# Fourier mixing folded over the model axis twice: smaller DFT products, the middle column apart

## The chip, the cores and the metric

The kernel runs on one core of a Trainium2 chip. The metric is device time in microseconds; it is compared over several runs of the same program. Engines are named as in the profile: PE (TensorE matmul) and PEld (its weight load), DVE (VectorE), ACT (ScalarE), POOL (GpSimd), SP (SyncE, here only a DMA queue).

## The reference

Eight batches of random-feature attention (8 heads, 576 rows, head size 64, 128 features), whose output x (8 x 576 x 512) goes through Fourier mixing, a layer norm and two channel products.

```python
q_p, k_p = phi(q * scale), phi(k * scale)       # phi: exp(h - max(h)), h = x @ omega.T - |x|^2 / 2
kv  = einsum('bhsm,bhsd->bhmd', k_p, v);  z = sum(k_p, axis=2)
x   = (q_p @ kv) / (q_p @ z + 1e-6)             # heads side by side: (8, 576, 512)
u   = x + real(fft(fft(x, axis=1), axis=2))
un  = (u - mean(u)) / sqrt(var(u) + 1e-6)
out = u + maximum(un @ w_ch1, 0) @ w_ch2        # 512 -> 2048 -> 512
```

The real part of the two-dimensional transform of a real x is C x C' - S x S', where C and S are the cosine and sine matrices over the sequence, and C' and S' those over the model axis. Cosines are even and sines odd in their index, both over the sequence (t and 576 - t) and over the model axis (d and 512 - d).

## The kernel before, in words

**Layout.** x of a batch is one tile of 97 partitions x 6 x 512. Sequence rows are kept as pairs: three chunks of "lo" rows t = 0 to 288 and three of "hi" rows 576 - t, chunks sharing their border rows. So x[:, 0:3] + x[:, 3:6] is the even part over the sequence and x[:, 0:3] - x[:, 3:6] the odd one.

**Stages of a batch.** `attn` computes four pairs of heads in 32 steps; its last step writes x's last columns from ndp (line 299). `mix` follows in 13 steps. For each block of 128 columns (dc = 0 to 3), DVE makes the even fold and POOL the odd one (line 321), six matmuls multiply them with the sequence tables cs and sn (yp, line 326, N = 289), and ACT copies the result to y (line 333). Then, for each of three chunks of rows, eight matmuls multiply y with the model tables cd and sd (ab, line 343, N = 257): only the columns 0 to 256 are computed, A from the even part and B from the odd part, since A - B is the transform at column k and A + B the one at 512 - k. ACT copies B (line 352), DVE forms A - B and A + B (lines 353, 354), POOL adds them to x (lines 358, 359; the right half reads them backwards), DVE and POOL make the layer norm (lines 363 to 371), PE transposes the rows (tp, line 382) and turns the hi rows round (fp, line 396). `mlp` runs the two channel products twice per batch, over lo and over hi rows: hp (line 411) and op (line 430), all with N = 289; then it transposes back (otp, line 446), adds (line 452) and stores.

**Order of the work.** The functions are generators. `together` advances the channel products of batch b as the main line, in 38 steps, and the attention and mixing of batch b + 1 beside it, in 45 steps (32 + 13), so that the mixing falls to the second half of the hi products: there each main step is a group of 8 op matmuls. Before that, the weights are loaded (64 pieces, given as doubles and narrowed to f32 by DVE and POOL, their DMAs issued from POOL's queue), with the attention and mixing of batch 0 beside them. The last batch's channel products have nothing beside them. Instructions keep this order by priority, each engine running its own queue in order; where an instruction isn't ready by the planner's own estimate, a later one is taken ahead.

**Buffers.** Scratch tiles are handed out from pools by tag. The fold tile before uses the tag "ke" of the attention (2 buffers), which "un" uses too; y is one buffer; the tiles of the hidden layer, ht, have 18 buffers, 16 of which one half-batch fills.

Of the kernel before, what the change touches and what calls it, by code (L numbers as in the profile page):

```python
# [12 lines left out]
AF = mybir.ActivationFunctionType  # L13
ALU = mybir.AluOpType
# [19 lines left out]
def _tables(S, DM):  # L34
    """The DFT matrices in the layouts of the two contractions."""
# [8 lines left out]
    d = 128 * np.arange(DM // 128)[None, :] + np.arange(128)[:, None]  # L44
    turn = (d[:, :, None] * np.arange(DM // 2 + 1)) % DM
    ang = 2.0 * np.pi * turn / DM
    cd = np.cos(ang)
    sd = np.where(turn * 2 % DM == 0, 0.0, np.sin(ang))
# [7 lines left out]
def kernel(  # L56
# [20 lines left out]
    KD = DM // 2 + 1  # L77
    R = 6
# [3 lines left out]
    # Both feature maps carry 1 / sqrt(MF); left out of both, it scales the term  # L82
    # that is added to the denominator.
# [68 lines left out]
        # the magnitude, within the range of float32  # L152
# [4 lines left out]
        # exponent - 1023 + 127 in eight bits  # L157
# [24 lines left out]
    # omega^T, once for each head of a pair  # L182
# [32 lines left out]
    def attn(b):  # L215
        x = xs[b] = xp.tile([CP, R, DM], F32, name="x", tag="x")
        for pr in range(NP):
# [9 lines left out]
            # q in the order of the pairs: lo t = 0 .. 288, hi t = 0 .. 288  # L227
# [37 lines left out]
            for i in range(2):  # L265
# [38 lines left out]
                )  # L304
                yield

# [1 line left out]
    uns = {}  # L308

    def mix(b):  # L310
# [207 lines left out]
```

## Time and profile before

| | |
|---|---|
| time, median of 3 runs (lowest to highest) | 1860.35 us (1859.08 to 1861.77) |
| span of the profiled execution (its only time shown) | 1856.5 us |
| instructions | 21861 |
| PE busy | 1752.1 us (94%), 9137 matmul instructions |
| PEld busy | 1409.8 us (76%) |
| DVE busy | 639.6 us (34%) |
| ACT busy | 358.2 us (19%) |
| POOL busy | 208.7 us (11%) |
| mean granted PE clock | 0.969 |

A row of the groups reads: line, engine, operation, out <- in by tile names, shapes, count, busy time and mean duration in ns, then the engine's idle time just before these instructions and what ended it. A row of the timeline reads: start, length, engine, line, operation, how many instructions are merged, and the idle time before. Matmuls are pipelined, so that durations overlap; distances between starts give the pace. Pool spans are rough.

### The profile page before, as it was taken

How to read it: one execution, taken by the hardware profiler on the slowest of the kernel's cores; microseconds unless marked ns; L12 is line 12 of the kernel's file. 1: busy time of each engine (PE TensorE's matmuls, PEld its weight loads, DVE VectorE, ACT ScalarE, POOL GpSimd, SP SyncE). 2: the span in 40 equal slices, each digit the busy share in tenths (PEclk: the TensorE clock that was granted, in tenths of full speed). 3: DMA queues.
4: the chain of work that ended last, by engine and by line, in shares of the span. 5: the costliest groups of instructions: out<-in, count | busy, mean ns of one | idle time of the engine just before them, and what ended most of it. 6: DMA issues, size and time to landing. Idle time of an engine off the chain costs nothing.

```text
span 1856.5 us, 21861 instructions
## 1 busy us (share of the span) xinstructions
PE 1752.1 (94%) x9137; PEld 1409.8 (76%) x9137; DVE 639.6 (34%) x1450; ACT 358.2 (19%) x641; POOL 208.7 (11%) x319
## 2 busy tenths in 40 slices
PE   5997988999999899999999999998999999998998
PEld 5885766877888688877888678886888778886776
DVE  5777873313242323313233132413233132332000
ACT  1221121112121212212221121212122121211100
POOL 2335331010001200011001100012000110012000
PEclk9997978999999999999999999999999999999999
DMA  6322322001110101101010011101011010000000
GB/s 145 82 79 71 93 76 55 7 1 26 26 45 7 26 20 29 24 7 26 20 40 20 9 24 23 43 7 26 20 33 26 1 26 20 20 1 13 1 13 13
DMA packets 125013, 57.73 MB, mean 31 GB/s; under 512 B 115762, under 2 KB 115762, under 8 KB 124916
## 3 DMA queue, kind: packets, MB, share of 16 engines
q1 hardware_dynamic: 119248, 37.83, 8.7%
q0 software_dynamic: 5120, 16.78, 2.8%
q10 hardware_dynamic: 548, 1.73, 0.4%
q8 instruction: 73, 1.20, 0.3%
q14 instruction: 24, 0.20, 0.0%
HBM read 46.88 MB, written 9.44 MB: 30 GB/s over the span
## 4 chain that ended last, share of the span: by engine, by line
PE 82%; DVE 7%; POOL 4%; DMA 4%; issue 2%; ACT 1%; POOLq 0%; SPq 0%; DVEq 0%; ACTq 0%
PE hp L411 26%; PE op L430 24%; PE yp L326 5%; PE kvp L269 5%; PE kp L245 4%; PE qp L254 4%; PE ndp L295 4%; PE ab L343 4%; DMA raw<-in_moe_w_ch_dram 4%; PE eps L280 2%; POOL x L359 1%; PE fp L396 1%; PE tp L382 1%; PE tps L194 1%; PE otp L446 1%
## 5 line engine op out<-in xcount | busy, mean ns | idle before, releaser
L430 PE MATMUL op<-ht,w 128*128 128x289 f32 x2048 | 531.7, 413 | 8.2 <-POOL w L170 8.2
L411 PE MATMUL hp<-unT,w 128*128 128x289 f32 x2048 | 532.5, 414 | 0.0
L430 PEld LDWEIGHTS op<-ht,w 128*128 128x128 f32 x2048 | 387.5, 192 | 116.9 <-POOL w L170 9.5
L411 PEld LDWEIGHTS hp<-unT,w 128*128 128x128 f32 x2048 | 387.0, 193 | 114.7 <-issue 8.7
L420 DVE TENSOR_SCALAR ht<-hp 128x289 f32<-128x289 f32 x128 | 58.8, 459 | 374.6 <-PE hp L411 374.6
L254 PE MATMUL qp<-omT,qT 64*97 64x128 f32 x768 | 112.1, 299 | 15.8 <-DVE qT L238 14.6
L245 PE MATMUL kp<-omT,kT 64*96 64x128 f32 x768 | 114.5, 302 | 5.3 <-DVE ke L206 2.9
L254 PEld LDWEIGHTS qp<-omT,qT 64*97 64x97 f32 x768 | 100.5, 182 | 22.8 <-issue 15.9
L245 PEld LDWEIGHTS kp<-omT,kT 64*96 64x96 f32 x768 | 98.5, 180 | 25.4 <-issue 17.9
L422 ACT ACTIVATE ht<-hp 128x289 f32<-128x289 f32 x128 | 52.8, 412 | 296.7 <-PE hp L411 296.7
L269 PEld LDWEIGHTS kvp<-v,ke 96*128 96x128 f32 x768 | 103.5, 209 | 6.9 <-issue 1.1
L269 PE MATMUL kvp<-v,ke 96*128 96x65 f32 x768 | 105.3, 291 | 0.0
L212 ACT ACTIVATE ke<-ke 96x768 f32<-96x768 f32 x64 | 53.8, 841 | 213.5 <-DVE ke L206 213.5
L295 PEld LDWEIGHTS ndp<-kv,qeT 128*97 128x97 f32 x768 | 82.3, 180 | 10.3 <-ACT qeT L286 2.0
L353 DVE TENSOR_TENSOR bmp<-ab,bmp 97x257 f32<-97x257 f32 x24 | 10.2, 423 | 221.4 <-ACT bmp L352 221.4
L204 DVE TENSOR_REDUCE kemx<-kp 96x6 f32<-96x768 f32 x64 | 60.8, 950 | 70.4 <-PE kp L245 70.4
L295 PE MATMUL ndp<-kv,qeT 128*97 128x65 f32 x768 | 82.6, 262 | 1.6 <-DVE kv L277 1.3
L452 DVE TENSOR_TENSOR x<-x,otp 97x512 f32<-97x512 f32 x48 | 32.5, 683 | 148.6 <-PE otp L446 148.6
L113 POOL MEMSET v<- 96x12 f32 x32 | 3.7, 116 | 700.6 <-PE kvp L269 694.0
L286 ACT ACTIVATE qeT<-eps 128x582 f32<-128x582 f32 x64 | 42.0, 656 | 192.9 <-PE eps L280 174.2
L321 POOL TENSOR_TENSOR fold<-x 97x384 f32<-97x384 f32 x32 | 40.1, 1252 | 331.7 <-PE kvp L269 242.2
L440 ACT ACTIVATE ot<-op 128x289 f32<-128x289 f32 x64 | 26.4, 412 | 255.4 <-PE op L430 255.4
(65 smaller groups left out, 1558.8 us busy)
## 6 DMA issues: line engine op xcount, KB each, us to landing
raw<-in_moe_w_ch_dram POOLq DMA_DIRECT2D x64, 256.0 KB, 3.0
kn<-in_k_dram SPq DMA_DIRECT2D x64, 144.0 KB
qn<-in_q_dram SPq DMA_DIRECT2D x64, 144.0 KB
v<-in_v_dram SPq DMA_DIRECT2D x64, 144.0 KB
out_dram<-x SPq DMA_DIRECT2D x40, 192.0 KB
out_dram<-x SPq DMA_DIRECT2D x8, 190.0 KB
cd_sb<-k_cd ACTq DMA_DIRECT2D x1, 385.5 KB
sd_sb<-k_sd ACTq DMA_DIRECT2D x1, 385.5 KB
```

What stands on the lines that cost most here:

```text
L204: nc.vector.tensor_reduce(mx[:], pr4, axis=AX.X, op=ALU.max)
L212: nc.scalar.activation(out=e[:], in_=e[:], func=AF.Exp, scale=SCALE)
L245: nc.tensor.matmul(kp[0:PR, r // 3, r % 3 * MF : r % 3 * MF + MF], lhsT=kT[rows, r, :], rhs=omT[rows, :],)
L254: nc.tensor.matmul(qp[0:CP, r // 3, r % 3 * MF : r % 3 * MF + MF], lhsT=qT[rows, t0 : t0 + CP], rhs=omT[rows, :],)
L269: nc.tensor.matmul(kvp[:, 0 : D + 1], lhsT=kes[i][:, r, :], rhs=v1[:, i, r, :], start=(r == 0), stop=(r == R - 1),)
L295: nc.tensor.matmul(nd[:, r, :], lhsT=qeT[:, r, :], rhs=kv[:])
L326: nc.tensor.matmul(yp[:, 0:NK], lhsT=f[:, c, :], rhs=tab[:, c, :], start=(c == 0), stop=(c == NC3 - 1),)
L343: nc.tensor.matmul(ab[0:CP, n, 0:KD], lhsT=y[:, n, dc, CW * c : CW * c + CP], rhs=tab[:, dc, :], start=(dc == 0), stop=(dc == NDC - 1),)
L411: nc.tensor.matmul(hp[:, 0:NK], lhsT=w1[:, dc, 128 * fc : 128 * fc + 128], rhs=un_t[:, dc, :], start=(dc == 0), stop=(dc == NDC - 1),)
L420: nc.vector.tensor_scalar(ht[:], hp[:, 0:NK], 0.0, None, op0=ALU.max)
L422: nc.scalar.activation(out=ht[:], in_=hp[:, 0:NK], func=AF.Relu)
L430: nc.tensor.matmul(op_[:, 0:NK], lhsT=w2[:, fc, 128 * dc : 128 * dc + 128], rhs=hs[fc][:], start=(fc == 0), stop=(fc == NFC - 1),)
```

## The change

The model axis is folded as well, and twice. First, the even part over the sequence is added to its mirror image over the model axis (columns 1 to 255 with 511 to 257), and the odd part has its mirror image subtracted: this leaves 257 columns. Second, column d is combined with column 256 - d, once added and once subtracted: one combination is enough for the even result columns k, the other for the odd ones. So there are four folds of 128 columns (n = 0 to 3: cosine for even k, cosine for odd k, sine for even k, sine for odd k), and both contractions run over 128 columns instead of 512.

- The sequence products become 4 x 3 matmuls of N = 289 instead of 8 x 3.
- The model products become, per chunk, one matmul each for A and B and for even and odd k, of N = 129 or 128 and without accumulation, instead of eight of N = 257.
- Column 128 is its own partner (256 - 128) in the second fold. For the sine part it takes the place of column 0 (which is zero there). For the cosine part it is carried apart in `mid_t`, multiplied with cs in three matmuls of N = 1 per chunk, and lands in column 257 of the sine bank; it is added to A for k a multiple of 4 and subtracted for k = 2 modulo 4.
- The tables cd and sd have their columns sorted (k = 0 mod 4, 2 mod 4, odd) and 128 rows instead of 512. DVE puts the columns back in order as it forms A - B and A + B: six instructions with strided results instead of two.
- The folds of a batch are now made at once, on the whole x: first all of DVE's, then all of POOL's, in two steps; the sequence products follow in two more steps, so that the count of 13 stays. Both engines use the one buffer of the scratch tile "half".
- ht has 17 buffers instead of 18, and fold has a buffer of its own.

```diff
-    d = 128 * np.arange(DM // 128)[None, :] + np.arange(128)[:, None]
-    turn = (d[:, :, None] * np.arange(DM // 2 + 1)) % DM
-    ang = 2.0 * np.pi * turn / DM
-    cd = np.cos(ang)
-    sd = np.where(turn * 2 % DM == 0, 0.0, np.sin(ang))
+    d = np.arange(DM // 4)[:, None]
+    k = np.arange(DM // 2 + 1)
+    k = np.concatenate([k[k % 4 == 0], k[k % 4 == 2], k[k % 2 == 1]])[None, :]
+    turn = (d * k) % DM
+    cd = np.cos(2.0 * np.pi * turn / DM)
+    turn = (np.where((d == 0) & (k % 2 == 1), DM // 4, d) * k) % DM
+    sd = np.where(turn * 2 % DM == 0, 0.0, np.sin(2.0 * np.pi * turn / DM))
...
+    QD = DM // 4
+    KE = QD + 1
+    K0 = DM // 8 + 1
...
-        y = fft.tile([128, 2, NDC, NK], F32, name="y", tag="y")
-        for dc in range(NDC):
-            cols = slice(128 * dc, 128 * dc + 128)
-            fold = att.tile([CP, 2, NC3, 128], F32, name="fold", tag="ke")
-            for n, (tab, eng, op) in enumerate(
-                ((cs, nc.vector, ALU.add), (sn, nc.gpsimd, ALU.subtract))
-            ):
-                f = fold[:, n]
+        fold = fft.tile([CP, NC3, 4, QD], F32, name="fold", tag="fold")
+        mid_t = small.tile([CP, NC3, 1], F32, name="mid", tag="mid", bufs=2)
+        for n, (eng, op, back) in enumerate(
+            ((nc.vector, ALU.add, ALU.add), (nc.gpsimd, ALU.subtract, ALU.subtract))
+        ):
+            h = fft.tile([CP, NC3, DM], F32, name="half", tag="half")
+            eng.tensor_tensor(out=h[:], in0=x[:, 0:NC3, :], in1=x[:, NC3:R, :], op=op)
+            eng.tensor_tensor(
+                out=h[:, :, 1 : 2 * QD],
+                in0=h[:, :, 1 : 2 * QD],
+                in1=h[:, :, DM - 1 : 2 * QD : -1],
+                op=back,
+            )
+            even, odd = (ALU.subtract, ALU.add) if n else (ALU.add, ALU.subtract)
+            for m, o in ((0, even), (1, odd)):
                 eng.tensor_tensor(
-                    out=f, in0=x[:, 0:NC3, cols], in1=x[:, NC3:R, cols], op=op
-                )
-                yp = sml.tile([128, 512], F32, name="yp", tag="sml")
-                for c in range(NC3):
-                    nc.tensor.matmul(
-                        yp[:, 0:NK],
-                        lhsT=f[:, c, :],
-                        rhs=tab[:, c, :],
-                        start=(c == 0),
-                        stop=(c == NC3 - 1),
-                    )
-                nc.scalar.activation(out=y[:, n, dc, :], in_=yp[:, 0:NK], func=AF.Copy)
+                    out=fold[:, :, 2 * n + m, :],
+                    in0=h[:, :, 0:QD],
+                    in1=h[:, :, 2 * QD : QD : -1],
+                    op=o,
+                )
+            middle = fold[:, :, 3, 0:1] if n else mid_t[:]
+            eng.tensor_copy(out=middle, in_=h[:, :, QD : QD + 1])
             yield
+
+        y = fft.tile([128, 4, NK], F32, name="y", tag="y")
+        for n, tab in enumerate((cs, cs, sn, sn)):
+            yp = sml.tile([128, 512], F32, name="yp", tag="sml")
+            for c in range(NC3):
+                nc.tensor.matmul(
+                    yp[:, 0:NK], lhsT=fold[:, c, n, :], rhs=tab[:, c, :],
+                    start=(c == 0), stop=(c == NC3 - 1),
+                )
+            nc.scalar.activation(out=y[:, n, :], in_=yp[:, 0:NK], func=AF.Copy)
+            if n % 2:
+                yield
...
             ab = big_tile("ab")
+            rows = slice(CW * c, CW * c + CP)
             for n, tab in enumerate((cd, sd)):
-                for dc in range(NDC):
+                for m, cols in enumerate((slice(0, KE), slice(KE, KD))):
                     nc.tensor.matmul(
-                        ab[0:CP, n, 0:KD],
-                        lhsT=y[:, n, dc, CW * c : CW * c + CP],
-                        rhs=tab[:, dc, :],
-                        start=(dc == 0),
-                        stop=(dc == NDC - 1),
-                    )
-            bmp = att.tile([CP, 3, KD], F32, name="bmp", tag="qe")
+                        ab[0:CP, n, cols], lhsT=y[:, 2 * n + m, rows], rhs=tab[:, cols]
+                    )
+            for i in range(NC3):
+                nc.tensor.matmul(
+                    ab[0:CP, 1, KD : KD + 1], lhsT=cs[:, i, rows], rhs=mid_t[:, i, :],
+                    start=(i == 0), stop=(i == NC3 - 1),
+                )
+            bmp = att.tile([CP, 3, KD + 1], F32, name="bmp", tag="qe")
             bs, mi, pl = (bmp[:, n, :] for n in range(3))
-            nc.scalar.activation(out=bs, in_=ab[0:CP, 1, 0:KD], func=AF.Copy)
-            nc.vector.tensor_tensor(out=mi, in0=ab[0:CP, 0, 0:KD], in1=bs, op=ALU.subtract)
-            nc.vector.tensor_tensor(out=pl, in0=ab[0:CP, 0, 0:KD], in1=bs, op=ALU.add)
+            nc.scalar.activation(out=bs, in_=ab[0:CP, 1, 0 : KD + 1], func=AF.Copy)
+            mid = bmp[:, 0, KD : KD + 1]
+            for dst, op in ((mi, ALU.subtract), (pl, ALU.add)):
+                for first, c0, c1, sign in ((0, 0, K0, ALU.add), (2, K0, KE, ALU.subtract)):
+                    nc.vector.scalar_tensor_tensor(
+                        dst[:, first:KD:4], ab[0:CP, 0, c0:c1], mid, bs[:, c0:c1], op0=sign, op1=op
+                    )
+                nc.vector.tensor_tensor(
+                    out=dst[:, 1:KD:2], in0=ab[0:CP, 0, KE:KD], in1=bs[:, KE:KD], op=op
+                )
...
-                ht = mlpp.tile([128, NK], F32, name="ht", tag="ht", bufs=NFC + 2)
+                ht = mlpp.tile([128, NK], F32, name="ht", tag="ht", bufs=NFC + 1)
```

More of the change, by code (lines that the diff above doesn't have):

```diff
@@ new lines, in mix @@
+        for n, tab in enumerate((cs, cs, sn, sn)):
+            yp = sml.tile([128, 512], F32, name="yp", tag="sml")
+            for c in range(NC3):
+                nc.tensor.matmul(
+                    yp[:, 0:NK],
+                    lhsT=fold[:, c, n, :],
+                    rhs=tab[:, c, :],
+                    start=(c == 0),
+                    stop=(c == NC3 - 1),
+                )
+            nc.scalar.activation(out=y[:, n, :], in_=yp[:, 0:NK], func=AF.Copy)
+            if n % 2:
+                yield
@@ L357, in mix @@
                 u = x[:, NC3 * g + c, :]
-                nc.gpsimd.tensor_tensor(out=u[:, 0:KD], in0=u[:, 0:KD], in1=left, op=ALU.add)
+                nc.gpsimd.tensor_tensor(out=u[:, 0:KD], in0=u[:, 0:KD], in1=left[:, 0:KD], op=ALU.add)
                 nc.gpsimd.tensor_tensor(
```

5 lines of the change are left out of this document (added).

## The prediction, made blind

> **What bounds the kernel now.** I read the page first: span, utilisation in 40 slices, granted clock, and the shares of the chain that ended last.
>
> ```profile
> span 1856.5 us, 21861 instructions
> PE   5997988999999899999999999998999999998998
> PEclk9997978999999999999999999999999999999999
> PE 82%; DVE 7%; POOL 4%; DMA 4%; issue 2%; ACT 1%; POOLq 0%; SPq 0%; DVEq 0%; ACTq 0%
> ```
>
> TensorE holds 82% of the chain, and from the eighth slice on it is nearly always busy. So I cut the span where the first product hp of a batch starts, and asked for busy time by stretch (columns: us, then busy time of PE, PEld, DVE, ACT, POOL, granted clock, DMA share, GB/s).
>
> ```profile
> 431.51:646.43 214.92, 209.69 (x1143) 168.69 (x1143) 63.33 (x125) 44.57 (x80) 14.92 (x23) 0.98 0.09 23
> 1506.52:1720.83 214.31, 205.31 (x1107) 164.84 (x1107) 60.76 (x119) 42.72 (x77) 14.34 (x21) 0.99 0.05 12
> 1720.83:1856.50 135.67, 129.66 (x537) 100.58 (x535) 11.30 (x22) 10.49 (x25) 0.00 (x0) 0.98 0.03 9
> ```
>
> A period of 215 us is one batch's channel products with attention and mixing of the next woven in; PE idles some 5 us of it. The mixings of batches 1 to 7 lie in seven such channel products (the first of these, before 431.51, is partly bound by weights); batch 0's lies in the weight loading; the last 136 us hold none. Then I read one mixing in order of time, PE only (start, us, instruction, idle time before it).
>
> ```profile
> 577.63 1.17 PE L295 MATMUL ndp<-kv,qeT 128*97 128x65 f32 x12
> 578.64 1.68 PE L326 MATMUL yp<-cs_sb,fold 97*128 97x289 f32 x6
> 581.62 4.06 PE L430 MATMUL op<-ht,w 128*128 128x289 f32 x16
> 585.51 1.63 PE L326 MATMUL yp<-cs_sb,fold 97*128 97x289 f32 x6
> 586.98 1.63 PE L326 MATMUL yp<-sn_sb,fold 97*128 97x289 f32 x6
> 588.45 4.06 PE L430 MATMUL op<-ht,w 128*128 128x289 f32 x16
> ...
> 605.99 1.90 PE L343 MATMUL ab<-cd_sb,y 128*97 128x257 f32 x8
> 607.73 1.90 PE L343 MATMUL ab<-sd_sb,y 128*97 128x257 f32 x8
> 609.47 4.54 PE L430 MATMUL op<-ht,w 128*128 128x289 f32 x18
> 615.63 1.01 PE L382 MATMUL tp<-ident,un 97*128 97x97 f32 x8 [1.61 <-DVE un L371]
> ...
> 630.44 0.52 PE L382 MATMUL tp<-ident,un 97*128 97x97 f32 x4 [1.71 <-DVE un L371]
> 630.80 0.60 PE L446 MATMUL otp<-ident,ot 128*97 128x128 f32 x4
> 631.24 0.60 PE L343 MATMUL ab<-cd_sb,y 128*97 128x257 f32 x2
> ...
> 642.86 1.55 PE L382 MATMUL tp<-ident,un 97*128 97x97 f32 x8 [0.41 <-DVE un L371]
> ```
>
> Two things are to be seen. The mixing's matmuls run back to back with the op groups, so a matmul taken out shortens the period. And behind each ab PE waits for the layer norm: ab's end at 609.47 to tp at 615.63 is 6.16 us of ACT, DVE and POOL work, which 18 op matmuls don't quite cover.
>
> **The pace of PE.** Durations in the groups overlap, so I take starts. The source has 96 yp matmuls with cs (4 column blocks, 3 chunks, 8 batches) and the trace 192, so each f32 matmul is two instructions:
>
> ```profile
> L326 PE MATMUL yp<-cs_sb,fold 97*128 97x289 f32 x192 | 54.1, 418 | 0.0
> ```
>
> 12 yp from 585.51 to 588.45: 0.245 us each (N=289). 16 ab from 605.99 to 609.47: 0.2175 (N=257). Four otp, 97 weight columns and N=128, from 630.80 to 631.24: 0.110. Twelve ndp, 97 weight columns and N=65, from 577.63 to 578.64: 0.084.
>
> **Removed and added on PE, per mixing.** yp goes from 24 matmuls to 12: 24 instructions x 0.245 = 5.9 us saved. ab goes from 24 matmuls (48 x 0.2175 = 10.4 us) to 12 of N=128 or 129 (24 x 0.110 = 2.6 us) and 9 of N=1 for the middle column. N=1 is not in the trace. From below it can't cost less than nothing; from above I bound it by ab's own 0.2175; I take 0.084, since ndp is the nearest row in weight columns and smallest in N: 18 x 0.084 = 1.5 us (0 to 3.9). Net: 5.9 + 10.4 - 2.6 - 1.5 = **12.2 us**.
>
> **The folds.** DVE's and POOL's rows, then their range (min/median/max ns):
>
> ```profile
> 579.26 0.56 DVE L299 TENSOR_TENSOR x<-ndp,rden 97x384 f32<-97x384 f32 x1
> 581.89 0.56 DVE L321 TENSOR_TENSOR fold<-x 97x384 f32<-97x384 f32 x1 [2.07 <-PE yp L326]
> 588.70 0.56 DVE L321 TENSOR_TENSOR fold<-x 97x384 f32<-97x384 f32 x1 [6.25 <-PE yp L326]
> 610.09 0.43 DVE L353 TENSOR_TENSOR bmp<-ab,bmp 97x257 f32<-97x257 f32 x1 [20.83 <-ACT bmp L352]
> 610.43 0.41 DVE L354 TENSOR_TENSOR bmp<-ab,bmp 97x257 f32<-97x257 f32 x1
> 581.92 1.39 POOL L321 TENSOR_TENSOR fold<-x 97x384 f32<-97x384 f32 x1 [6.97 <-PE yp L326]
> 133.67 1.00 POOL L321 TENSOR_TENSOR fold<-x 97x384 f32<-97x384 f32 x1
> L321 POOL TENSOR_TENSOR fold<-x x32: 995/1370/1496, 112.6 to 1663.8; 97x384 f32<-97x384 f32 x32
> L358 POOL TENSOR_TENSOR x<-x,bmp x48: 629/635/1755, 147.8 to 1714.0; 97x257 f32<-97x257 f32 x48
> L206 DVE TENSOR_TENSOR qe<-qp,qemx 97x768 f32<-97x768 f32 x64 | 60.9, 951 | 0.9
> L277 DVE COPY kv<-kvp 128x65 f32<-128x65 f32 x64 | 14.4, 226 | 58.0 <-PE kvp L269 58.0
> ```
>
> Before, four folds of 384 columns ran on each engine, the first ones while the last heads were still computed. Now each engine has 1536 + 765 + 384 + 384 = 3069 columns and a tiny copy, and can begin only when the last head's x is written (579.82). DVE: 0.56 us for 384 and 0.95 for 768 give 1.02 ns per column, so 1.73 + 0.95 + 2 x 0.56 + 0.15 = 3.9 us: done at 583.7. The scratch tile "half" has one buffer, so POOL waits for DVE's last read of it, then needs 8 x 1.0 + 0.1 = 8.1 us at the 0.995 us pace (8 x 1.50 = 12 at the slowest row of L321): done at 591.8.
>
> When does PE ask? By the alternation of 38 main and 45 other steps, DVE's fold comes right after ndp, then op x16, POOL's fold, op x16, the cs products, op x16, the sn products. With 3.89 us per op group and 2.94 for six matmuls: cs at 578.64 + 7.78 = 586.4 (DVE is 2.7 us early), sn at 586.4 + 2.94 + 3.89 = 593.25 (POOL is 1.4 us early). I cost the folds at **nothing**; three op groups cover them. Without cover the sn products would wait; at 12 us POOL ends at 595.7, 2.5 us late.
>
> I take 1.0 rather than 1.37 us for a POOL fold because the 1.39 us row starts 0.03 us after DVE's fold and outlasts it, and now POOL starts when DVE has finished. The Trainium skill (SBUF — State Buffer, section "SBUF: two separate sides") says that DVE with two SBUF inputs and GpSimd take a shared port pair in turn for whole instructions, the loser blocked. By that rule POOL's instructions, the longest some 4 us, would block DVE; in this stretch DVE has nothing from 589.26 to 610.09, so the sum would be the same here, and dearer only among the weight conversions. The trace agrees with the blocking (1.39 beside DVE, 1.00 alone).
>
> **Behind ab.** mi and pl become six DVE instructions of 65, 64 and 128 columns. L353 to L354 starts 0.34 us apart; a 65-column copy lasts 0.226 us, so mi takes some 0.45 to 0.65 us instead of 0.34, and pl hides behind POOL's first add. I charge 0.2 us a chunk, 0.6 per mixing (-0 to +1.5), all of it on the layer-norm chain that PE already waits for. ACT's copy gains one column; POOL's adds keep their size. ht with 17 buffers instead of 18 costs nothing: an hp group needs the buffer whose last op matmul came at least 15 matmuls earlier on PE.
>
> **Batch 0 and the start.** Rows: the first 20 us, a table load, and the wait at the end of the weights.
>
> ```profile
> 0.00:20.00 20.00, 5.50 (x25) 4.60 (x25) 3.73 (x15) 3.06 (x4) 3.33 (x13) 1.00 1.06 211
> cd_sb<-k_cd ACTq DMA_DIRECT2D x1, 385.5 KB
> cd_sb<-k_cd ACTq DMA_DIRECT2D x1, 128.5 KB
> 292.81 18.87 PE L430 MATMUL op<-ht,w 128*128 128x289 f32 x68 [4.19 <-POOL w L170]
> ```
>
> PE waits for the last weights at 292.81, so what mixing 0 saves is hidden; it counts as nothing (12 if not). The weight stream passes through DVE, POOL and POOL's DMA queue in order, and POOL's long folds now stand in front of its next raw load: 8.1 instead of 4.6 us of POOL, 1.7 more of DVE, and a wait of up to 4 us for "half" while nothing is issued behind it. Against that, cd and sd shrink from 1028 to 257 KB in a stretch that moves 211 GB/s, worth 3.7 us. I take +3 us (-4 to +9).
>
> **Sum.** 1856.5 - 7 x 12.2 + 7 x 0.6 + 3 = 1778.3 us of span. The median run of 1860.35 lies 3.85 us above the span, taken to stay (no separate time of the profiled execution is shown): **1782 us**, 4.2% less.
>
> **Rivals.**
> (a) *Another half-clock stretch.* Near the end of each period the clock falls for 6.8 us:
>
> ```profile
> 641.90:648.70 6.80, 6.36 (x19) 3.95 (x18) 3.59 (x5) 3.04 (x5) 0.32 (x1) 0.51 0.06 13
> ```
>
> It follows the gaps around tp and the thin attention matmuls. Shorter ab groups bring the idle gaps closer together; one more such stretch costs up to 3.4 us of PE work per period, 7 x 3.4 = 24: 1806. Against it: the gaps of 1.6 and 1.7 us stand at full clock now. Beside that row, the Trainium skill (TensorE: Matmul & The Clock Gate, section "HAM oscillation — how this bites in real kernels") says that idle gaps longer than a window of about 3.4 us bring the half rate back; by that rule gaps near 2 us bring no further stretch.
> (b) *POOL becomes the bound, mildly:* 1.37 to 1.50 us per 384 columns, sn products 1.5 to 2.5 us late, or N=1 at 0.2175 (2.4 us): 11 to 17 us, 1793 to 1799.
> (c) *More gain:* the thin ab of the third chunk fits whole into the 1.7 us wait before 630.44, its layer norm starts earlier, and some 2.5 us of the 5 us idle time go too: 7 x 2.5 = 17, 1765.
> (d) *Slower:* the sn products wait for POOL in every batch. L358's slowest row, 1755 ns for 257 columns, is 6.8 ns a column; at that pace 3069 columns take 21 us, POOL ends at 604.7, and PE waits 11.5 us, all that is saved. From there on the kernel is slower, 1862 to 1875. Only rows among weight conversions are so slow.
> (e) *No gain:* the layer-norm chain, not PE, sets the period; then nothing moves: 1860. The op groups at zero idle time speak against it.
>
> **Chances.** Forecast 0.55 (own range 1768 to 1796), (a) 0.15, (b) 0.12, (c) 0.10, (d) 0.05, (e) 0.03. The range holds the forecast, (b), (a) and nearly (c): 1764 to 1816. A measurement here tells about 0.2% (4 us) from no change; faster 0.92, same 0.03, slower 0.05.
>
> **What would show it.** Period near 203.4 us instead of 215; yp x12 in 2.94 us twice per mixing; ab of a chunk in 1.4 us; DVE's fold some 4 us and POOL's 8 us, over before the first sn product, with no PE wait there. Wrong: a PE wait for POOL at yp, a second stretch at 0.5 clock per period, N=1 matmuls over 0.1 us apart, or the last weights later than 300 us.

## The result, and the profile after

| | before | after |
|---|---|---|
| time, median (lowest to highest) | 1860.96 us (1859.08 to 1861.77, 4 runs) | 1751.54 us (1749.84 to 1754.09, 4 runs) |
| span of the profiled execution | 1856.5 us | 1748.5 us |
| PE busy | 1752.1 us | 1648.2 us |

The ratio is 0.9417, with a 95% interval of 0.9404 to 0.9430. The gain of 109 us is larger than the 79 us forecast, and the time lies 12 us below the range given. The direction was right and the size was not. So the question is where the other 30 us came from.

The page of the kernel after, with the same rows as before: the span, PE's busy tenths, the granted clock, and the shares of the chain that ended last.

```profile
span 1748.5 us, 21376 instructions
PE   6976888999999999999999999999999999998998
PEclk9995887999999999999999999999999999999999
PE 82%; DVE 8%; POOL 4%; DMA 3%; issue 1%; ACT 1%; POOLq 0%; DVEq 0%; ACTq 0%
```

TensorE still holds 82% of the chain. The profile does not point to another engine; it is the same bound with less of it.

Next, busy time by stretch, cut where the first hp of a batch starts. Before, the five periods from batch 1 to batch 6 together:

```profile
431.31:1506.31 1075.00, 1048.58 (x5712) 843.33 (x5711) 316.60 (x625) 222.88 (x400) 74.30 (x115) 0.98 0.09 23
```

After, the same five periods, the sixth, and one stretch at half clock:

```profile
416.37:1413.51 997.14, 976.88 (x5561) 795.90 (x5560) 330.06 (x691) 213.57 (x380) 88.87 (x120) 1.00 0.10 25
1413.51:1613.48 199.97, 192.48 (x1077) 156.03 (x1076) 63.35 (x133) 40.95 (x73) 17.52 (x22) 0.99 0.05 13
812.84:816.26 3.42, 3.25 (x6) 1.75 (x7) 1.86 (x3) 1.63 (x4) 0.00 (x0) 0.50 0.24 60
```

The whole gain of 108.0 us of span can be read from these rows. The first hp of batch 1 starts at 416.37 instead of 431.31: 14.9. Five periods of 199.43 instead of 215.00: 5 x 15.57 = 77.9. The sixth, 199.97 instead of 214.32: 14.3. From there to the end, 135.02 instead of 135.87: 0.9.

So a period lost 15.6 us, where the sum had 11.6 (12.2 of work, less 0.6). PE's busy time per period fell from 209.72 to 195.38 us, its idle time from 5.28 to 4.05. Full clock came back too. In the trace's record of the granted clock, which holds only 1.0 and 0.5 (half clock below), each of the five periods before holds one stretch of 6.8 us at 0.5. After, there are two stretches of 3.4 us in all five together.

One mixing after, PE only, in order of time (start, us, instruction, idle time before it):

```profile
561.60 1.16 PE L304 MATMUL ndp<-kv,qeT 128*97 128x65 f32 x12
562.60 8.01 PE L470 MATMUL op<-ht,w 128*128 128x289 f32 x32
570.44 3.09 PE L352 MATMUL yp<-cs_sb,fold 97*128 97x289 f32 x12
573.37 4.06 PE L470 MATMUL op<-ht,w 128*128 128x289 f32 x16
577.27 3.09 PE L352 MATMUL yp<-sn_sb,fold 97*128 97x289 f32 x12
580.20 4.06 PE L470 MATMUL op<-ht,w 128*128 128x289 f32 x16
584.09 0.60 PE L371 MATMUL ab<-cd_sb,y 128*97 128x129 f32 x4
584.53 0.60 PE L371 MATMUL ab<-sd_sb,y 128*97 128x129 f32 x4
584.97 0.59 PE L376 MATMUL ab<-mid,cs_sb 97*97 97x1 f32 x6
585.43 5.11 PE L470 MATMUL op<-ht,w 128*128 128x289 f32 x20
591.95 1.01 PE L422 MATMUL tp<-ident,un 97*128 97x97 f32 x8 [1.41 <-DVE un L411]
...
597.95 4.14 PE L470 MATMUL op<-ht,w 128*128 128x289 f32 x16
601.92 0.60 PE L371 MATMUL ab<-cd_sb,y 128*97 128x129 f32 x4
602.37 0.60 PE L371 MATMUL ab<-sd_sb,y 128*97 128x129 f32 x4
604.56 0.53 PE L422 MATMUL tp<-ident,un 97*128 97x97 f32 x4 [1.59 <-DVE un L411]
...
611.56 1.52 PE L263 MATMUL qp<-omT,qT 64*97 64x128 f32 x12 [0.68 <-DVE rstd L406]
...
615.14 15.79 PE L451 MATMUL hp<-unT,w 128*128 128x289 f32 x64
```

Three things are to be seen. The sequence products take 2.93 us (570.44 to 573.37), twice per mixing, with no wait. A chunk's model products take 1.34 us (584.09 to 585.43), and the six N=1 instructions 0.46 of it, 0.077 us each. From the end of the last op group (601.92) to the first hp (615.14) PE has 13.2 us of narrow matmuls and short waits. Before, that stretch ran from 628.14 to 646.23, or 18.1 us, and its last part was at half clock (start, us, instruction; kernel before):

```profile
628.14 0.60 PE L343 MATMUL ab<-cd_sb,y 128*97 128x257 f32 x2
640.65 1.79 PE L254 MATMUL qp<-omT,qT 64*97 64x128 f32 x12 [1.03 <-DVE qT L238]
644.44 1.99 PE L396 MATMUL fp<-x,flip 97*97 97x512 f32 x2
646.23 4.02 PE L411 MATMUL hp<-unT,w 128*128 128x289 f32 x11
```

The folds after, on DVE and then on POOL:

```profile
563.82 1.76 DVE L329 TENSOR_TENSOR half<-x 97x1536 f32<-97x1536 f32 x1
567.54 0.16 DVE L345 COPY mid<-half 97x3 f32<-97x3 f32 x1
567.78 3.43 POOL L329 TENSOR_TENSOR half<-x 97x1536 f32<-97x1536 f32 x1 [10.22 <-DVE mid L345]
573.19 1.96 POOL L338 TENSOR_TENSOR fold<-half 97x384 f32<-97x384 f32 x2
575.21 0.19 POOL L345 COPY fold<-half 97x3 f32<-97x3 f32 x1
```

DVE takes 3.9 us and is done 2.7 us before the cosine products start; POOL takes 7.6 us and is done 1.9 us before the sine products start (its first sine fold, which is all that the first of these products needs, 3.1 us before). PE's waits for the folds, over the whole execution (in total, times, longest):

```profile
PE yp L352 <- DVE fold L338: 8.4, 1, 8.4
PE yp L352 <- POOL fold L338: 2.9, 1, 2.9
```

Once each, in batch 0; in no later batch.

### The profile page after: what moved, and what is told of

It reads as the page before. It is cut to its first block, busy times and chain, and to the rows that moved or that the text cites. A ratio compares the mean times of both kernels' runs of the same rounds, so it can differ in the third digit from the quotient of the medians.

```text
span 1748.5 us, 21376 instructions
## 1 busy us (share of the span) xinstructions
PE 1648.2 (94%) x8897; PEld 1341.4 (77%) x8897; DVE 664.4 (38%) x1554; ACT 343.7 (20%) x609; POOL 233.2 (13%) x327
## 4 chain that ended last, share of the span: by engine, by line
PE 82%; DVE 8%; POOL 4%; DMA 3%; issue 1%; ACT 1%; POOLq 0%; DVEq 0%; ACTq 0%
PE hp L451 27%; PE op L470 25%; PE kvp L278 5%; PE qp L263 5%; PE kp L254 5%; PE ndp L304 4%; DMA raw<-in_moe_w_ch_dram 3%; PE yp L352 3%; PE eps L289 2%; DVE st L403 2%; POOL x L399 2%; PE tps L203 1%; PE otp L486 1%; PE fp L436 1%; PE tp L422 1%
## 5 line engine op out<-in xcount | busy, mean ns | idle before, releaser
L451 PEld LDWEIGHTS hp<-unT,w 128*128 128x128 f32 x2048 | 382.7, 191 | 113.7 <-issue 6.4
L389 DVE SCALAR_TENSOR_TENSOR bmp<-ab,bmp 97x65 f32<-97x65 f32 x96 | 25.7, 328 | 175.2 <-ACT bmp L385 175.2
L179 POOL TENSOR_TENSOR w<-ta,rest 128x256 f32<-128x256 f32 x64 | 53.8, 840 | 171.1 <-DVE rest L176 171.1
```

What stands on the lines that cost most here:

```text
L179: nc.gpsimd.tensor_tensor(out=dst, in0=ta[:].bitcast(F32), in1=rest[:], op=ALU.add)
L451: nc.tensor.matmul(hp[:, 0:NK], lhsT=w1[:, dc, 128 * fc : 128 * fc + 128], rhs=un_t[:, dc, :], start=(dc == 0), stop=(dc == NDC - 1),)
```

## The experiments

All were timed in the same way, each beside runs of the kernel before on the same chip (medians 1859.4 to 1861.3 us). In the table, "period" is the mean of the five periods from the first hp of batch 1 to that of batch 6; busy and idle are PE's in it, and "half clock" is the time per period at 0.5 in the trace's record of the granted clock.

| kernel | time, us | period | busy | idle | half clock |
|---|---|---|---|---|---|
| before | 1861 | 215.00 | 209.72 | 5.28 | 6.8 |
| sequence products halved (e1) | 1822.6 | 209.56 | 204.62 | 4.94 | 8.2 |
| model products small (e2) | 1840.1 | 211.77 | 206.02 | 5.74 | 11.8 |
| after | 1751.5 | 199.43 | 195.38 | 4.05 | 1.4 |
| after, statistics twice (e4) | 1803.0 | 206.85 | 200.83 | 6.02 | 13.7 |
| after, over 36 steps (e8) | 1781.2 | 203.41 | 198.67 | 4.74 | 8.9 |
| the same with wide filler (f) | 1783.7 | 203.14 | 199.13 | 4.02 | 1.4 |
| before, over 32 steps (g) | 1856.2 | 214.27 | 209.15 | 5.13 | 2.7 |
| after, over 32 steps (g) | 1756.1 | 200.37 | 195.77 | 4.60 | 0.0 |
| after, chunks overlapped, 34 steps (h) | 1716.3 | 194.22 | 194.10 | 0.12 | 0.0 |
| before, chunks overlapped, 34 steps (i) | 1795.2 | 206.17 | 206.05 | 0.12 | 0.0 |
| h, but the first batch over 38 steps (h2) | 1716.9 | 193.52 | 193.41 | 0.12 | 0.0 |
| after, POOL's fold longer (e3) | 1808.7 | 206.64 | 198.78 | 7.86 | 8.6 |
| after, no N=1 matmuls (e9) | 1751.0 | 199.15 | 195.41 | 3.75 | 4.7 |

**Each half of the change alone, in the kernel before.** First the sequence products: two of four column blocks are left out.

```diff
         for dc in range(NDC):
...
+                if dc > 1:
+                    continue
                 yp = sml.tile([128, 512], F32, name="yp", tag="sml")
...
-                        lhsT=y[:, n, dc, CW * c : CW * c + CP],
+                        lhsT=y[:, n, dc % 2, CW * c : CW * c + CP],
```

> The kernel before with half of the sequence products: the blocks dc = 2 and 3 are folded but not multiplied (24 of 48 yp instructions per mixing go; the model products keep their count and size, and read blocks 0 and 1 twice, so the output is another one). Theory W (work, and a tail behind the third ab): only the yp work goes, 24 x 0.245 = 5.9 us per period, and the half-clock stretch and the waits behind the third ab stay; 7 x 5.9 = 41, so 1820 us and a period of 209.1. Rival F (the surplus of some 3.3 us per period comes from the sequence side, folds that no longer wait for buffers): 9 us per period, so 1797 and a period of 206.

Measured: 1822.6 us (1821.2 to 1824.21), ratio 0.9789 (0.9775 to 0.9804), 38.7 us less. Its five periods:

```profile
428.20:1475.99 1047.79, 1023.09 (x5592) 823.98 (x5591) 316.88 (x625) 215.20 (x380) 74.72 (x115) 0.98 0.10 23
```

The forecast price of the sequence products, 7 x 5.9 = 41 us, holds to within 3 us: the work is on PE's path. Rival F, 1797, is out.

Then the model products:

```diff
-                for dc in range(NDC):
+                for dc, cols in enumerate((slice(0, 129), slice(129, KD))):
                     nc.tensor.matmul(
-                        ab[0:CP, n, 0:KD],
+                        ab[0:CP, n, cols],
                         lhsT=y[:, n, dc, CW * c : CW * c + CP],
-                        rhs=tab[:, dc, :],
-                        start=(dc == 0),
-                        stop=(dc == NDC - 1),
+                        rhs=tab[:, dc, cols],
                     )
...
+            for i in range(NC3):
+                nc.tensor.matmul(
+                    ab[0:CP, 1, KD : KD + 1], lhsT=cs[:, i, CW * c : CW * c + CP],
+                    rhs=mhalf[:, 0:1], start=(i == 0), stop=(i == NC3 - 1),
+                )
...
```

> The kernel before with the model products of the changed one: four matmuls of N = 129 or 128 and three of N = 1 per chunk instead of eight of N = 257 (blocks dc = 2 and 3 are left out of them, so the output is another one); folds and sequence products as before. Theory W: ab's own 48 x 0.2175 - 24 x 0.110 - 18 x 0.077 = 6.4 us per period and beside it the surplus of some 3.3 us, since the tail behind the third ab shrinks by more than its matmuls and the half-clock stretch goes: 9.7 us, 7 x 9.7 = 68, so 1793 and a period of 205.3. Rival F: 6.4 us alone, 1816 and a period of 208.6, with the half-clock stretch still there.

Measured: 1840.1 us (1839.11 to 1840.46), ratio 0.9881 (0.9865 to 0.9898). Both theories missed, by 24 us and more. Its five periods:

```profile
433.32:1492.16 1058.84, 1030.12 (x5682) 834.14 (x5681) 318.28 (x625) 223.48 (x400) 77.23 (x115) 0.97 0.10 23
```

Some 6.3 us of work left each period (10.4 - 2.6 - 1.5, as in the prediction), but busy time fell by only 3.7, and the half-clock time rose from 6.8 to 11.8 us per period. By the price of half clock worked out below, some 0.45 us for each us, that rise is 2.3 us, most of what is missing. The two halves alone bring 39 + 21 = 60 us, together 109. The clock doesn't add up part by part, and it can go either way.

**A longer layer norm, in the kernel after.** The row statistics on DVE are taken twice.

```diff
+                nc.vector.bn_stats(out=st[:], in_=u)
                 nc.vector.bn_stats(out=st[:], in_=u)
```

> The changed kernel with each bn_stats of the layer norm made twice (the same result): DVE's part of the chain between ab and tp grows by up to 1.38 us a chunk. Theory W with PE waiting for this chain in each of the three chunks: 3 x 1.3 = 3.9 us per period, 27 us, so 1779; if the longer waits bring the half-clock stretch back, 2.3 us per period more, 1795. Rival P (PE alone is the bound and the waits are slack that other work would fill): no change beyond 4 us, 1752 to 1756.

Measured: 1803.0 us (1797.9 to 1806.11), ratio 0.9681 (0.9661 to 0.9702).

```profile
422.74:1457.00 1034.26, 1004.17 (x5561) 814.45 (x5560) 347.54 (x720) 215.21 (x380) 89.11 (x120) 0.97 0.10 24
```

The layer-norm chain is on the path, but only 2.0 of the 7.4 us per period are idle time. The other 5.4 are busy time at unchanged matmuls, and half-clock time rose from 1.4 to 13.7 us per period. The expectation that named the half clock (1795) came nearest and was still too low.

**Where the narrow matmuls fall.** Next came the order. In the kernel after, the 45 steps of attention and mixing are handed out over 36 main steps instead of 38.

```diff
-            together(mlp(b), run(attn(b + 1), mix(b + 1)), N_MLP, N_NEXT)
+            together(mlp(b), run(attn(b + 1), mix(b + 1)), N_MLP - 2, N_NEXT)
```

> The changed kernel with the attention and mixing of the next batch handed out over the first 36 instead of all 38 main steps, so that two more main steps lie behind the third ab and cover its layer norm. Theory W: of the 4.06 us that PE waits in a period, the part in the tail and part of the two others go, 1.5 to 2.5 us per period, so 1735 to 1741. Rival P: the waits only move, 1750 to 1754.

Measured: 1781.2 us (1778.86 to 1784.91), ratio 0.9569 (0.9554 to 0.9584): both theories had expected the time of the kernel after or less, and it is 30 us more.

```profile
428.28:1445.34 1017.06, 993.34 (x5561) 806.35 (x5561) 329.69 (x690) 215.37 (x381) 88.91 (x120) 0.98 0.10 24
```

The matmuls are the same 5561, and idle time rose by 0.7 us per period; busy time rose by 3.3, with half-clock time at 8.9 us. Another 11.9 us were lost ahead of batch 1's first hp (428.28 instead of 416.37); why is not shown. In the timeline of PE (start, us, instruction) it shows on a single row: the same twelve qp, 1.52 us in the kernel after, take nearly twice as long here.

```profile
625.01 2.83 PE L263 MATMUL qp<-omT,qT 64*97 64x128 f32 x12 [1.06 <-DVE qT L247]
```

To take the half clock away at that place, I put four wide matmuls among the third chunk's transposes of this kernel. Their result goes nowhere.

```diff
+            if c == NC3 - 1:
+                dm = sml.tile([128, 512], F32, name="dm", tag="sml")
+                for j in range(4):
+                    nc.tensor.matmul(dm[:, :], lhsT=w1[0:CP, 0, 0:128], rhs=x[:, c, :])
```

> The changed kernel with the hand-out over 36 main steps (which took 1781 us, with half-rate stretches of 6.8 to 10 us in each period) and four more matmuls of N = 512 that nobody reads, just before the third chunk's transposes: 8 instructions, some 3.5 us of PE work per mixing, set where PE waits and runs thin matmuls. Theory C: the half-rate stretches go (some 3.6 us per period), the added work fills 2 to 2.5 us of waiting; it ends at 1757 to 1768 though it does 24 us more work. Rival O (the order costs the 30 us): 1788 to 1805.

Measured: 1783.7 us (1783.04 to 1785.99), ratio 0.9589 (0.9575 to 0.9603). Its five periods, then the filler in the timeline of PE (eight instructions):

```profile
427.15:1442.87 1015.72, 995.64 (x5602) 799.66 (x5601) 331.08 (x690) 215.33 (x381) 88.75 (x120) 1.00 0.10 24
```

```profile
623.55 3.70 PE L412 MATMUL dm<-x,w 97*128 97x512 f32 x8 [0.37 <-POOL x L399]
```

The half clock went, from 8.9 to 1.4 us per period, with work added rather than removed. The time stayed, because the filler's 3.5 us of PE work cost what the clock gave back. Neither expectation had the time right; the clock moved as the clock theory said. As the filler also fills part of a wait (idle time fell by 0.7 us), this run alone doesn't tell narrow matmuls from waits.

Then both kernels with the 45 steps over 32 main steps, so that the mixing ends among channel products and not behind them:

```diff
-            together(mlp(b), run(attn(b + 1), mix(b + 1)), N_MLP, N_NEXT)
+            together(mlp(b), run(attn(b + 1), mix(b + 1)), N_MLP - 6, N_NEXT)
```

> The kernel before with the next batch's attention and mixing handed out over the first 32 of the 38 main steps: the same instructions, but all three ab chunks stand among op groups and no thin stretch of small matmuls lies before the next batch's hp. Theory C (the clock: a stretch of thin attention matmuls and waits behind the third ab makes PE run at half rate for 6.8 us in each period of the kernel before, and the change gained its work plus the end of these stretches): the half-rate stretch goes, 3.4 us per period; the waits stay, three of some 1.8 us; 7 x 3.4 = 24, so 1837. Rival O (the order behind the third ab, not the clock, made the surplus): 1855 to 1865, or slower.

> The changed kernel with the same hand-out over 32 main steps. Theory C: PE's work is that of the changed kernel, no half-rate stretches, three waits of 6.5 - 20 x 0.2435 = 1.6 us instead of 4.06 us in all: 1748 to 1757. Against the kernel before with the same hand-out the difference is then the work alone, 7 x 12.2 less the longer chain: 80 to 86 us, not 109. Rival O: the difference stays at 105 to 110.

Measured: 1856.2 us for before (1851.52 to 1860.74, ratio 0.9981, 0.9967 to 0.9994) and 1756.1 for after (1754.68 to 1758.83, ratio 0.944, 0.9426 to 0.9454). The time for before is a miss of theory C (1837) and lies in the range of rival O; the time for after lies in theory C's range. The distance is 100 us, between the two theories. The five periods of the one, then of the other:

```profile
430.23:1501.59 1071.36, 1045.73 (x5712) 836.11 (x5711) 321.64 (x626) 224.35 (x400) 74.62 (x115) 0.99 0.09 23
```

```profile
415.89:1417.75 1001.86, 978.86 (x5562) 791.84 (x5561) 334.37 (x691) 216.06 (x380) 88.77 (x120) 1.00 0.10 24
```

This order removed most or all of the half clock but kept the waits. In before the half-clock time fell by 4.1 us per period and the busy time by only 0.6, so this order costs PE time in another way, which I did not find. It doesn't isolate the work.

**Work alone: no waits, no half clock.** Each chunk's part of the mixing was cut in two. The front runs from the model products to rstd, and the back holds un and the transposes. The next chunk's front now comes ahead of the back of the chunk before; the 45 steps go over 34 main steps.

```diff
-        for c in range(NC3):
+        def front(c):
...
+            norms[c] = mv, rstd
             yield
+        def back(c):
+            mv, rstd = norms[c]
...
+        norms = {}
+        for part in (front(0), front(1), back(0), front(2), back(1), back(2)):
+            yield from part
...
-            together(mlp(b), run(attn(b + 1), mix(b + 1)), N_MLP, N_NEXT)
+            together(mlp(b), run(attn(b + 1), mix(b + 1)), N_MLP - 4, N_NEXT)
```

> The changed kernel with the hand-out over 34 main steps, and in the mixing the ab of the next chunk before the transposes of the one before it, so that two op groups (7.8 us) stand between ab and its tp. Theory C: the 6.5 us chain is covered, and 4.06 us of waiting per period go without a half-rate stretch: 7 x 4 = 28 below the changed kernel, 1724. If waits cost nothing because other work fills them: 1750.

Measured: 1716.3 us (1714.53 to 1717.22), ratio 0.9223 (0.9209 to 0.9237). It is the fastest version here, 35 us below the kernel after and 8 us below theory C's 1724; that waits cost nothing (1750) is out. Its five periods, then its timeline of PE behind one ab:

```profile
414.93:1386.02 971.09, 970.50 (x5563) 791.92 (x5562) 333.14 (x691) 213.42 (x380) 88.76 (x120) 1.00 0.10 25
```

```profile
578.49 4.14 PE L478 MATMUL op<-ht,w 128*128 128x289 f32 x16
582.47 0.50 PE L426 MATMUL tp<-ident,un 97*128 97x97 f32 x4
```

No wait stands before a tp, and PE is idle for only 0.12 us per period. The kernel before was then given the same two edits:

> The kernel before, with two edits of order: the next chunk's model products are issued ahead of the transposes of the chunk before, and the 45 steps are handed out over 34 main steps. The same two edits had left the changed kernel with no wait and no half clock after the weights (period 194.2 us, 1716 us). Theory C (the change's gain is 12.2 us of TensorE work per mixing, and the other 3 us per period are waits and half-clock time that went with the old order): here, too, waits and half clock go, the period is 194.2 + 12.2 = 206.4 us, the time about 1861 - 6 x 8.5 + 8 = 1818 at the least favourable and 1800 at the best; the distance to the changed kernel with the same edits is about 7 x 12.2 = 85 us. Rival O (the change takes more than 12.2 us of work off TensorE): the distance stays 100 to 109 us, so 1816 to 1825, with a period near 209.

Measured: 1795.2 us (1794.43 to 1795.57), ratio 0.9653 (0.9636 to 0.9669).

```profile
420.79:1451.62 1030.83, 1030.24 (x5713) 833.75 (x5712) 316.31 (x626) 221.71 (x400) 74.34 (x115) 1.00 0.10 24
```

This pair separates the terms. With waits and half clock gone from both, a period is 206.17 against 194.22 us, **11.95 us of work per mixing** where the prediction had 12.2. Theory C's period was 206.4; a period near 209, and with it the rival that the change takes more than 12.2 us of work off TensorE (100 to 109 us in all), is out. The times are 79 us apart where 85 was expected, and 1795.2 is below the 1800 to 1818 named for this kernel. The six us that the distance lacks lie ahead of batch 1's first hp, which comes at 420.79 and 414.93, only 5.9 us apart.

**The cover of POOL's fold.** In the kernel after, POOL's first fold instruction is done three times.

```diff
             eng.tensor_tensor(out=h[:], in0=x[:, 0:NC3, :], in1=x[:, NC3:R, :], op=op)
+            if n:
+                for again in range(2):
+                    eng.tensor_tensor(out=h[:], in0=x[:, 0:NC3, :], in1=x[:, NC3:R, :], op=op)
```

> The changed kernel with POOL's first fold instruction (97x1536, 3.43 us) done three times: 6.9 us more on POOL in each mixing, TensorE's work and order unchanged. In the changed kernel POOL's even sine fold is done some 1.9 us before the sine products ask for it (cosine 2.7 us). Theory C: the cover ends there; the sine products wait 3 to 5 us in every period, 7 x 4 = 28, and the time is 1775 to 1785, more if the wait brings half-clock stretches back. Rival (the folds are covered by more than the distance read from the trace, or the planner moves channel products ahead): 1752 to 1756.

Measured: 1808.7 us (1806.65 to 1812.19), ratio 0.9727 (0.9708 to 0.9746). The sine products in the timeline of PE, then busy time in the stretch from their start on:

```profile
595.91 6.15 PE L355 MATMUL yp<-sn_sb,fold 97*128 97x289 f32 x12 [3.81 <-POOL fold L341]
```

```profile
595.91:602.74 6.83, 6.83 (x15) 4.87 (x16) 0.00 (x0) 0.82 (x2) 1.09 (x2) 0.51 0.00 0
```

The wait is 3.81 us, within the 3 to 5 worked out: 6.93 us more of POOL, less the 3.1 us by which its first sine fold was early. But behind it the clock is 0.51 for 6.83 us, and the same twelve matmuls take 6.15 instead of 3.09 us. A period grew by 7.2 us, 3.8 of it idle and 3.4 busy; another 13.8 us were lost ahead of batch 1's first hp (430.13 instead of 416.37). Here a wait costs nearly twice its length, and so the time is 24 us above the 1775 to 1785 expected without more half clock.

**The N=1 matmuls.** They are left out of the kernel after, so the middle column is missing from the result.

```diff
-            for i in range(NC3):
-                nc.tensor.matmul(ab[0:CP, 1, KD : KD + 1], lhsT=cs[:, i, rows], rhs=mid_t[:, i, :], ...)
...
```

> The changed kernel without the nine N=1 matmuls per mixing that bring in the middle column (the middle column of the cosine part is left out of the result; the six vector instructions take another column of the same size instead). Theory C: 18 instructions x 0.077 us = 1.4 us of TensorE work go per mixing, 7 x 1.4 = 10: 1742, if waits and half-clock time stay as they are; each 3.4 us stretch that comes or goes per period is worth 1.4 us x 7 = 10 more. Rival (the N=1 matmuls lie in the wait for the layer norm and cost nothing): 1752.

Measured: 1751.0 us (1747.17 to 1753.51), ratio 0.9413 (0.9395 to 0.9431): no change that could be told.

```profile
414.83:1410.60 995.77, 977.04 (x5471) 794.46 (x5470) 329.06 (x690) 213.65 (x380) 88.76 (x120) 0.99 0.10 25
```

The expected 10 us did not come, but not because the matmuls lie in a wait: then idle time would have grown by 1.4 us per period, and it fell by 0.3. PE's busy time stayed at 195.4 us with 90 instructions fewer, and half-clock time rose from 1.4 to 4.7 us per period. At 0.45 us each (below) that is 1.5 us, what the matmuls had cost. So 1.4 us of work bought nothing, as far as this price holds, and as the expectation's note on stretches allowed.

**The start.** The kernel with overlapped chunks gets its last weights some 10 us later than the kernel after. Does the hand-out beside the weight loading do that?

```diff
-            together(mlp(b), run(attn(b + 1), mix(b + 1)), N_MLP - 4, N_NEXT)
+            together(mlp(b), run(attn(b + 1), mix(b + 1)), N_MLP - (4 if b else 0), N_NEXT)
```

> The changed kernel with next chunk's model products ahead of the transposes of the chunk before, and the 45 steps over 34 main steps, but the first channel products (beside the weight loading) hand out over 38 as in the changed kernel. Theory C: the last weights come near 296 instead of 306 us, the periods stay at 194.2 us: 1716 - 10 = 1706. Rival (the late weights are from the new order of the mixing, not from the hand-out): 1716.

Measured: 1716.9 us (1714.89 to 1719.1), ratio 0.9232 (0.9217 to 0.9247), the same as without. The last weight is narrowed at 297.5 instead of 306.0 us, so the hand-out is the cause of most of the lateness, but batch 1's first hp comes at 416.4 instead of 414.9. The 8.5 us did not reach the end, and theory C's 1706 is a miss; the rival had the time right for a reason that the run refutes. That the first channel products of both versions have work enough to run beside the weights would explain it, but is not shown.

## Why the prediction was right and wrong, point by point

**Work taken off TensorE: right.** 12.2 us per mixing were worked out from distances between starts; the pair without waits shows 11.95. Term by term: twelve sequence instructions in 2.93 us (2.94 forecast), a chunk's model products in 1.34 (1.4), N=1 at 0.077 (0.084, bounds 0 to 0.22). That the 79 us between those two kernels equal the forecast of the whole is chance.

**The folds cost nothing: right.** DVE 3.9 us as forecast; POOL 7.6 (8.1 forecast) and done 1.9 us early (1.4 forecast). The longer fold shows that the cover ends where the rows said. Rival (d)'s deciding point was too far out, though: it charged a late POOL with the wait alone, where a wait of 3.8 us came to 7.2 us of the period.

**The start: smaller.** +3 us were charged for the weight stream. The run of 68 op matmuls at the end of the weights started at 292.81 before, behind a weight. In the chain that ended last of the kernel after (start, us, engine, instruction) it starts here, and what it follows is kp, no longer a weight:

```profile
293.36 18.77 PE op L470 x68
```

So the cost was about 0.5, inside its bounds of -4 to +9. The last weight, narrowed at 295.6, is inside the 300 us named. With the first period's full gain of 14.9 us this gave 6 us more than the forecast's 8.6.

**The layer-norm chain and the waits: wrong sign.** 0.6 us per period were added. The chain did get longer: ab's end to tp is 6.52 us (585.43 to 591.95) instead of 6.16, +0.36 a chunk where 0.2 was charged. But the planner put 20 instead of 18 op matmuls into it, and 8 of the third chunk's 14 model-product instructions went ahead of the second wait. So the two waits before tp shrank from 1.61 and 1.71 to 1.41 and 1.59 us, 0.3 in all; the other 0.9 went from the shorter waits among the narrow matmuls behind them. PE's idle time per period fell by 1.2 us instead of growing by 0.6: half of what rival (c) had, by (c)'s mechanism in part.

**The clock: the step that failed.** The sum took no term for the clock: it left the half-clock stretch of 6.8 us in every period as it was, at no cost and no gain, and rival (a) considered the clock only in the one direction, more of it. In fact the stretches nearly went: 6.8 to 1.4 us per period. What that is worth can be estimated across the table. Take full-rate busy time as 206.05 and 194.10 us from the pair without half clock, and 5.9, 6.3, 1.4 and 3.5 us for the matmuls that an experiment removes or adds. The excess of busy time over it is then, against half-clock time: after 1.3 to 1.4, e9 2.7 to 4.7, before 3.7 to 6.8, e1 4.5 to 8.2, e3 4.7 to 8.6, e8 4.6 to 8.9, e2 6.3 to 11.8, e4 6.7 to 13.7. A line through these has some 0.6 us and 0.45 us for each us at half clock; at a granted clock of 0.5, half of the time is the most that could be lost. The two kernels over 32 steps lie off it (1.7 and 3.1 us at 0 and 2.7), so this price is for kernels in the old order of steps.

The account of a period is then 11.95 of work, 0.45 x (6.8 - 1.4) = 2.4 of clock and 1.2 of idle time, 15.6 us as measured. The line was drawn with both kernels on it; drawn without them, it gives 2.5 for the clock. Against the 11.6 of the sum, the clock is 2.4 more, the waits 1.8 more (1.2 gained, 0.6 charged) and the work 0.25 less: 4.0 us, or 28 of the missing 30 over seven mixings. None of the four signs of being wrong that the prediction listed appeared in any period; all four were signs of a slower kernel.

**Rival (a) misread its own row.** It named both the gaps around tp and the thin matmuls ahead of the half clock, but worked out only what the gaps would do. Beside the row of 6.80 us at 0.51, the kernel before has no wait over 1.03 us behind the tp at 630.44, and the 3.4 us ahead of it hold that wait and narrow matmuls (kp and qp, 64 weight rows). The Trainium skill (TensorE: Matmul & The Clock Gate, section "HAM oscillation — how this bites in real kernels") speaks of idle gaps longer than about 3.4 us. The wait of 3.81 us in the kernel with the longer fold agrees with it; the stretch behind waits of at most 1.7 us does not, and there the measurement decides: a stretch of narrow matmuls with short waits was enough.

**What decides the half clock.** The traces narrow it. All half-clock stretches of an execution start on a grid of 3.413 us and last whole steps of it, but for the one that the end of the record cuts off (in the kernel before, 641.76 and 856.80 lie 215.04 apart, 63 steps). For each step, add up weight rows times N over the matmul instructions, one across a border by its share, in thousands. In the kernel after, the step with the least in each of the five narrow stretches holds 223, 185, 213, 176 and 216, and half clock follows only behind the 185 and the 176. PE's busy time does not sort them so. Here are a step before with less busy time, but of instructions with 128 weight rows (ab and otp, 213), and the step of the 185, mostly 64 rows (kp and qp):

```profile
1710.13:1713.55 3.42, 1.50 (x9) 1.04 (x7) 1.35 (x3) 0.39 (x1) 1.34 (x3) 1.00 0.20 58
809.43:812.84 3.41, 2.61 (x23) 2.08 (x21) 3.41 (x9) 0.46 (x2) 0.70 (x1) 1.00 0.59 140
```

Full clock stayed behind the first and half clock began behind the second. A limit of 192, set from the kernels before and after alone, from 312 us on (behind the weights), is wrong for 9 of the 5160 steps in the other twelve executions, of which 131 are followed by half clock; a limit on busy time, set in the same way, is wrong for 100. So what counts here is the matmul work in a step, and narrow instructions and waits both lower it. It also says why only two of five nearly equal periods had half clock: 199.43 us are 58.4 steps, so each period is cut in another place, while the 215.00 us before are 63.0 steps and every period was cut alike.

**What stays open.** This count was found in the traces afterwards, and no run was made to test it; in the first 140 us of each execution it does not hold, since the clock stayed full at smaller sums. Why each half of the change alone raised the half-clock time, while both together lowered it, is by this account a matter of how full the narrow stretch is and where the grid cuts it; no run isolates it. The 0.6 us of the line, and the time that the order over 32 steps costs, have no explanation.

## What to carry to other kernels

Where TensorE sets the period, cost a removed matmul from distances between starts, but then look at every half-clock stretch and ask whether it comes, goes or moves; here its coming and going was worth an estimated 2 to 5 us per period, against 12 us of work removed. A narrow stretch is at risk where weight rows times N add up to little over 3.4 us, even if PE looks busy. To measure work alone, first find an order in which both kernels have neither waits nor half clock, and take the difference there. That order was also the better kernel: issuing the next chunk's products ahead of the transposes that wait for the layer norm brought 35 us on top of the change.

## What the runs showed of the hardware that was not expected

- Half clock came without any long wait, behind narrow matmuls, in stretches of 3.4 us or whole multiples of it, and cost an estimated 0.45 us for each us.
- From 312 us on, half clock followed a step of 3.413 us in which weight rows times N came to less than some 195 thousand, for all but 6 of 6031 steps in the fourteen traces.
- A wait of 3.81 us for POOL was followed by 6.83 us at a clock of 0.51, and so cost about 7.2 us.
- Taking out 1.4 us of matmuls per mixing, or handing work out two steps earlier, changed the time by 0 and by +30 us; in the periods, most of that goes with the half-clock time (1.4 to 4.7 and to 8.9 us).
- A matmul instruction of N=1 with 97 weight columns took 0.077 us of PE's path, hardly less than the 0.084 of N=65.
